# Block 0 of a linear-attention and SwiGLU kernel: k^T v in two parts, and the first weight piece moved behind k, v and q

## The chip, the cores and the metric

The kernel runs on one core of a Trainium2 chip. The metric is the device time of one execution in microseconds (us). The kernel before took 1027.06 us (median of three runs, 1026.48 to 1028.2).

A core has a matrix engine (PE, with its weight loads shown apart as PEld), a vector engine (DVE), a scalar engine (ACT), a pool engine (POOL), and a queue engine (SP) that in this kernel only issues transfers. Each engine works through its own list of instructions in order. Matrix results land in PSUM, which is taken in banks of 128 partitions by 512 float32.

## The reference

```
kv  = einsum('bhsd,bhse->bhde', k, v)          # 8 batches, 8 heads, 576 tokens, 64 wide
out = einsum('bhsd,bhde->bhse', q, kv)
rms = sqrt(mean(out*out, axis=-1) + 1e-06)
x   = (out / rms * g_norm)  -> transposed to (4608, 512)
y   = (silu(x @ w_gate) * (x @ w_val)) @ w_out # d_ff 1536
```

q, k, v and g_norm are float32. The three weights are float64 and are rounded to float32 on the chip.

## The kernel before

The 4608 tokens are handled in nine blocks of 512. For each block the attention part makes `x`, and the feed-forward part multiplies it with the weights. PE is busy nearly all the time, and what block n+1 needs of the attention part is done while block n is multiplied. Block 0 has nothing before it to hide behind, so its attention part lies open at the start of the kernel. The change is in that start, which `Att.first` (line 459) writes out in order.

**Loads.** `load_q(0)` (line 290) sends half of q of block 0. `load_first_kv` (line 221) then sends k and v in two halves `g` of four heads each: 512 KB of k and 512 KB of v per half on SP's queue (line 230), and two small pieces of 64 KB per half on ACT's queue (line 233). Line 234, inside that loop, asks for one weight piece, so the first piece of `w_gate` (512 KB, line 135) goes out between the first and the second half. Then `load_q(1)` sends the other half of q, and `load_weights(4)` three more pieces. Below, k1, v1 and k2, v2 are the two halves, and wg0, wv0, wg1, wv1, ... are the weight pieces in order: there are 24 of `w_gate` and `w_val`, then 12 of `w_out` (line 1036). Every transfer on these queues is given one of eight completion semaphores in turn and waits until the transfer that had that semaphore before it has landed.

**Room for loads.** The pool `ld` has four tiles. q takes two of them for a while, the weight pieces turn round in all four. A piece's tile is free for the next load once ACT (line 160) and DVE (line 152) have read it.

**Rounding a piece.** `begin` issues one ACT instruction (line 146) and three on DVE (lines 147, 152, 153); `finish` one on ACT (line 160) and one on DVE (line 162). `weights(n)` (line 1048) rounds pieces up to n. In block 0, wg0 is rounded by `weights(1)` right after q's first transposes, wv0 begins at line 468 and ends in `weights(2)`, and wg1 and wv1 come from `weights(3)` and `weights(4)` later.

**The attention part of block 0.** `turn_q(0)` transposes two tiles of q on PE. `first_kv` (line 239) computes k^T v for the four pairs of heads j into two banks of the pool `m` with 72 matmuls; each operand has 64 rows, and the two halves of the 128 tokens go to different banks, so the two banks must be added. ACT copies the first bank (line 253) and DVE adds the second (line 254). `product(0)` multiplies q with the sum (line 356), 32 matmuls; `turn_q(1)`, `product(1)`, the squares on ACT (line 367), their sums on DVE (line 368), the inverse root (`root`, small DVE instructions), the scaling (`scale`, line 113) and the transposes of x (`turn_x`, lines 403 and 404) follow. `warm` (line 484) keeps PE busy meanwhile. `plain_up` (line 1011) then multiplies x with the weights, first only for half of the tokens (`plain_up(0, (0,))`), and for one column tile f after another.

**Order.** The body of the kernel is recorded by a layer that orders the instructions of each engine by a planner's own estimates; `tc.issue_after(i)` keeps what is inside from being placed before instruction i. When a matmul reads a weight tile of which another part is rounded, the layer orders the two as if they overlapped: the matmuls with rows i = 1 to 3 of wg0 are made to wait for wg1 if wg1's rounding was recorded first.

**Towards block 1.** Once the weight piece number 30 has been sent, the loads of k, v and q of block 1 follow on SP's queue (line 265 and the 32 small transfers of line 283). q is transposed by DVE (line 330), and block 1's `product` waits for that.

Of the kernel before, what the change touches and what calls it, by code (L numbers as in the profile page):

```python
# [8 lines left out]
F32 = mybir.dt.float32  # L9
# [5 lines left out]
P = 128  # L15
# [3 lines left out]
def kernel(  # L19
# [41 lines left out]
    nc = tc.nc  # L61

    B, H, S, D = q.shape
# [7 lines left out]
    NS = DM // P  # L71
# [22 lines left out]
    a_psum = pool("a_psum", 1, space=PS)  # L94
    b_psum = pool("b_psum", 3, space=PS)
    c_psum = pool("c_psum", 2, space=PS)
    m_psum = pool("m_psum", 2, space=PS)
# [8 lines left out]
    kvs = [consts.tile([P, NS, D], F32, name=f"kv{i}") for i in range(3)]  # L106
# [4 lines left out]
    add = lambda e, o, a, b: e.tensor_tensor(out=o, in0=a, in1=b, op=OP.add)  # L111
# [62 lines left out]
    words = {}  # L174
# [18 lines left out]
    class Att:  # L193
# [27 lines left out]
        def load_first_kv(self):  # L221


            room = self.room.rearrange("p f (h x) -> p (f h) x", h=2)
            most = {"k": room[:, 0:H], "v": room[:, H : 2 * H]}
            last = {x: room[:, 2 * H + i].rearrange("p (h d) -> p h d", d=D) for i, x in enumerate("kv")}
            for g in range(2):
                heads, rows = slice(NS * g, NS * (g + 1)), slice(D * g, D * (g + 1))
                for x, src in (("k", k), ("v", v)):
                    nc.sync.dma_start(  # L230
                        out=most[x][:, heads], in_=src[0, heads, 0:BLK].rearrange("h (p t) d -> p h (t d)", t=T)
                    )
                    nc.scalar.dma_start(out=last[x][rows], in_=src[0, heads, BLK:S].rearrange("h p d -> p h d"))
                load_weights(1)
            self.k, self.v = (
                [most[x].rearrange("p h (t d) -> p h t d", t=T)[:, :, t] for t in range(T)] + [last[x]] for x in "kv"
            )

        def first_kv(self):

            banks = [m_psum.tile([P, NS, D], F32, name="m") for _ in range(2)]
            for j in range(NS):
                g = j // 2
                for c in range(T + 1):
                    for r in range(2) if c < T else (g,):
                        for u in range(2):
                            h = 2 * j + u
                            k, v = (t[c][r * D : (r + 1) * D, h if c < T else h % NS] for t in (self.k, self.v))
                            nc.tensor.matmul(
                                banks[r][u * D : (u + 1) * D, j], lhsT=k, rhs=v, start=(c == 0),  # L250
                                stop=(c == (T if r == g else T - 1)),
                            )
            nc.scalar.copy(out=kvs[0], in_=banks[0])
            add(nc.vector, kvs[0], banks[1], kvs[0])

        def load_kv(self, g):

# [84 lines left out]
        def product(self, i, pools=None):  # L342

            pools = pools or (m_psum, m_psum)
            self.ps[i] = [pool.tile([P, 2, NS, D], F32, name=pool.name[0]) for pool in pools]
            for t in range(2):  # L350
                for j in range(NS):
                    for b, _, p0, p1 in self.parts(2 * i + t):
                        for p in range(p0, p1, D):
                            for u in range(2):
                                rows = slice(u * D, (u + 1) * D)
                                self.multiplied = nc.tensor.matmul(  # L356
                                    self.ps[i][u][p : p + D, t, j, :],
                                    lhsT=self.qt[rows, 2 * i + t, j, p : p + D], rhs=kvs[b % 3][rows, j, :],
                                    start=True, stop=True,
                                )  # L360
            if self.z is None or 0 < self.n < TURNED:
                self.z = st_pool.tile([P, 2, 2, 2, NS], F32, name="z")
            if i == 0:
                self.sq = ring().rearrange("p f (t j d) -> p f t j d", t=2, j=NS)
            for u in range(2):
                sq = self.sq[:, 2 * i + u]
                self.squared = nc.scalar.activation(out=sq, in_=self.ps[i][u], func=ACT.Square)
                self.summed = nc.vector.tensor_reduce(out=self.z[:, i, u], in_=sq, axis=mybir.AxisListType.X, op=OP.add)
# [89 lines left out]

        def first(self):
            self.turn_q(0, (b_psum, c_psum))  # L460
            weights(1)
            self.first_kv()
            self.product(0)
            with tc.issue_after(self.multiplied.ins):
                self.turn_q(1, (b_psum, c_psum))

            with tc.issue_after(self.copied_q.ins), tc.issue_after(self.summed.ins):
                begun = words[pieces[1]].begin()
            with tc.issue_after(begun.ins):
                self.product(1, (b_psum, a_psum))  # L470
            self.warm()
            self.root(0, 2)
            self.scale(0)
            with tc.issue_after(self.squared.ins), tc.issue_after(self.scaled.ins):
                weights(2)
            self.turn_x(0)
            self.scale(1)
            return self.squared, self.scaled
# [561 lines left out]
    def load_weights(upto):  # L1040
        nonlocal loaded, sent
        while loaded < min(upto, len(pieces)):
            load_w(*pieces[loaded])
            loaded += 1
            if loaded == len(pieces) - NP:
                sent = words[pieces[loaded - 1]].sent

    def weights(upto):
        nonlocal rounded
        while rounded < min(upto, len(pieces)):  # L1050
            load_weights(rounded + 4 if blocks[0].q[2:] else 1)
            round_w(*pieces[rounded])
            rounded += 1

# [13 lines left out]
    for n in range(NB):  # L1068
        ffn = Ffn(n, blocks[n])
        nxt = blocks[n + 1] if n + 1 < NB else None  # L1070
        if n == 0:

            with tc.issue_after(squared.ins), tc.issue_after(scaled.ins):
                weights(3)
            ffn.plain_up(0, (0,))
            copied = blocks[0].copied
            blocks[0].turn_x(1)
            for f in range(NF):
                with tc.issue_after(blocks[0].copied.ins if f else copied.ins):
                    weights(2 * (f + 2))  # L1080
                ffn.plain_up(f) if f else ffn.plain_up(0, (1,))
            weights(len(pieces))
            pairs = wo.rearrange("p (j e) d -> p e j d", e=2)
            t2(pairs[:, 0, :, HD:DM], pairs[:, 1, :, HD:DM], pairs[:, 0, :, 0:HD])
            nxt.room = x_pool.tile([P, 3, 7, P], F32, name="xi").rearrange("p a b c -> p (a b c)")

            with tc.issue_after(sent.ins):
                for i in range(2):
                    nxt.load_kv(i)
                for i in range(2):  # L1090
                    nxt.load_q(i)
            ffn.plain_end()
            for g in range(2):
                nxt.kv(g)
        else:

            def third():
                nxt.kv(0)
                nxt.load_kv(1)

            def two_thirds():
                nxt.kv(1)
                if nxt.n == 2:
                    for i in range(2):
                        nxt.load_q(i)

            fill = {4: third, 8: two_thirds} if nxt else {}
            if n == DEEP:
                for a, at in enumerate((1, 2, 3, 5)):
                    fill[at] = lambda i=a // 2, j=a % 2: nxt.load_quarters(i, (j,))  # L1110
            ffn.up(fill)
        if nxt:
            nxt.turn()
        if 0 < n < NB - 2:
            blocks[n + 2].load_kv(0)
        if DEEP <= n < NB - 2:
            for i in range(2):
                blocks[n + 2].load_q(i)
        ffn.down(nxt)
        if n == 0:  # L1120
            blocks[2].load_kv(0)

            with tc.issue_after(nxt.halves[0].ins):
                for j in range(NP // 2):
                    t2(wv[j][:, 0:2], wv[j][:, 2:4], wg[j][:, 0:2])
            with tc.issue_after(ffn.down_.s4.ins):
                for j in range(NP // 2, NP):
                    t2(wv[j][:, 0:2], wv[j][:, 2:4], wg[j][:, 0:2])
# [31 lines left out]
```

## Time and profile before

| what | value |
|---|---|
| median of three runs | 1027.06 us |
| the profiled execution, its own time | 1028.2 us |
| its span, first to last instruction | 1026.4 us |
| PE busy | 1007.2 us (98%) |
| DVE busy | 702.3 us (68%) |
| ACT busy | 228.1 us (22%) |
| PE idle, 0 to 42 us, for k and v | 7.0 us in two waits |
| PE idle, 0 to 42 us, for q | 4.9 us in two waits |
| PE starts the 512-wide matmuls of block 0 | 41.33 us |
| mean granted PE clock | 1.00 |

The profile has several views. The chain of waits follows the work that ended last back to its start. The timeline lists instructions in order of time: start, length, engine, line, operation, output<-input, a count, and in brackets how long the engine had been idle and what ended that. Rows with "SPq" or "ACTq" are the issuing of transfers. A view by tile gives the shortest, median and longest duration of each kind of instruction in ns. PE waits of the start are the only long ones of the execution; after 42 us PE waits for other engines 2.1 us in all.

### The profile page before, as it was taken

Reading aid. Unit: us, or ns where it says so; the run is one execution under the profiler, and the core shown is the slowest. Engines: PE = TensorE matmul, PEld = TensorE weight load, DVE = VectorE, ACT = ScalarE, POOL = GpSimd, SP = SyncE. Lnnn points to the kernel's source line nnn. Section 1 sums busy time; section 2 is a strip of 40 time slices with the busy share of each in tenths; the row PEclk is TensorE's granted clock in tenths of the full one; section 3 lists DMA queues with packets and bytes.
Section 4 is the critical chain, followed back from the end, with each engine's and each line's share of the span. In section 5 each row is a group of like instructions: output and inputs, shape, how many; then the busy total and the mean of one; then the engine's idle time right before and its main releaser. Section 6 shows DMA issues by size and latency. Waiting matters only on the chain.

```text
span 1026.4 us, 21403 instructions
## 1 busy us (share of the span) xinstructions
PE 1007.2 (98%) x8522; PEld 897.9 (87%) x8522; DVE 702.3 (68%) x1168; ACT 228.1 (22%) x352; POOL 368.9 (36%) x280
## 2 busy tenths in 40 slices
PE   5999999999999999999999999999999999999998
PEld 4544688888999989998999899988999999989997
DVE  2998788998665855685657566664669466856661
ACT  2665211221112212221121121111112111211110
POOL 0000253445045512562156314730455036513670
PEclk9999999999999999999999999999999999999999
DMA  8589553567888466845686468737872766067601
GB/s 229 184 254 257 117 99 121 156 158 181 240 229 233 88 155 199 251 110 116 201 241 156 78 204 239 195 54 194 235 197 49 180 194 186 22 162 210 188 30 42
DMA packets 273844, 170.26 MB, mean 166 GB/s; under 512 B 150608, under 2 KB 241872, under 8 KB 273744
## 3 DMA queue, kind: packets, MB, share of 16 engines
q1 hardware_dynamic: 238800, 164.42, 59.1%
q10 hardware_dynamic: 34880, 4.46, 2.7%
q8 instruction: 68, 1.11, 0.5%
q14 instruction: 32, 0.26, 0.1%
q0 software_dynamic: 64, 0.00, 0.0%
HBM read 138.02 MB, written 22.41 MB: 156 GB/s over the span
## 4 chain that ended last, share of the span: by engine, by line
PE 89%; DVE 6%; DMA 3%; SPq 1%; issue 1%; ACT 0%; ACTq 0%; DVEq 0%
PE b L716 26%; PE b L553 19%; PE c L716 13%; PE c L553 10%; PE a L716 6%; PE a L553 5%; PE b L1020 4%; PE c L1020 4%; DMA h<-in_v_dram 1%; PE m L356 1%; PE m L315 1%; DVE r L112 1%; DVE r L111 1%; DVE xi L112 1%; SPq L283 1%
## 5 line engine op out<-in xcount | busy, mean ns | idle before, releaser
L111 POOL TENSOR_TENSOR r<-r 128x256 f32<-128x256 f32 (+1 forms) x105 | 110.7, 1061 | 301.1 <-DVE r L111 272.4
L111 DVE TENSOR_TENSOR r<-b,r 128x512 f32<-128x512 f32 (+1 forms) x273 | 161.9, 606 | 65.6 <-PE b L716 60.6
L112 POOL TENSOR_TENSOR t<-wo 128x512 f32<-128x512 f32 x81 | 114.5, 1437 | 217.0 <-DVE wo L111 108.6
L111 DVE TENSOR_TENSOR r<-c,r 128x512 f32<-128x512 f32 (+1 forms) x179 | 108.5, 617 | 88.2 <-PE c L716 54.5
L716 PE MATMUL b<-x,t 128*128 128x128 f32 x1092 | 151.3, 276 | 0.0
L111 DVE TENSOR_TENSOR r<-a,r 128x512 f32<-128x512 f32 (+1 forms) x99 | 62.5, 631 | 113.4 <-PE a L553 71.1
L716 PEld LDWEIGHTS b<-x,t 128*128 128x128 f32 x1092 | 136.5, 192 | 0.8 <-DVE r L111 0.2
L716 PE MATMUL c<-xi,t 128*128 128x128 f32 x840 | 112.4, 276 | 0.4 <-DVE xi L111 0.4
L113 POOL TENSOR_TENSOR h<-r 128x1024 f32<-128x1024 f32 (+1 forms) x40 | 82.3, 2072 | 77.0 <-DVE r L111 74.1
L716 PEld LDWEIGHTS c<-xi,t 128*128 128x128 f32 x840 | 102.9, 192 | 0.5 <-DVE xi L111 0.5
L553 PE MATMUL b<-wo,h 128*128 128x256 f32 x432 | 100.1, 383 | 0.1
L553 PE MATMUL b<-t,h 128*128 128x256 f32 x432 | 96.9, 381 | 0.0
L553 PEld LDWEIGHTS b<-t,h 128*128 128x128 f32 x432 | 81.6, 190 | 11.3 <-issue 0.2
L553 PEld LDWEIGHTS b<-wo,h 128*128 128x128 f32 x432 | 79.9, 190 | 13.1 <-DVE h L113 2.5
L730 ACT COPY r<-b 128x512 f32<-128x512 f32 x63 | 36.9, 585 | 211.6 <-PE b L716 206.5
L716 PE MATMUL b<-xi,t 128*128 128x128 f32 x588 | 79.8, 276 | 0.0
L716 PEld LDWEIGHTS b<-xi,t 128*128 128x128 f32 x588 | 72.4, 192 | 0.0
L716 PE MATMUL b<-x,wg 128*128 128x128 f32 x336 | 52.7, 279 | 0.2 <-DVE x L112 0.2
L716 PE MATMUL b<-x,wv 128*128 128x128 f32 x336 | 51.4, 276 | 0.0
L553 PE MATMUL a<-wo,h 128*128 128x256 f32 x216 | 48.3, 379 | 0.0
L553 PE MATMUL c<-wo,h 128*128 128x256 f32 x216 | 48.1, 379 | 0.0
L553 PE MATMUL c<-t,s 128*128 128x256 f32 x216 | 48.1, 379 | 0.0
(128 smaller groups left out, 1560.7 us busy)
## 6 DMA issues: line engine op xcount, KB each, us to landing
t<-w SPq DMA_DIRECT2D x336, 256.0 KB, 3.6
out_dram<-r SPq DMA_DIRECT2D x17, 512.0 KB, 3.1
ld<-in_k_dram SPq DMA_DIRECT2D x26, 288.0 KB, 4.9
ld<-in_v_dram SPq DMA_DIRECT2D x26, 288.0 KB, 6.1
ld<-in_moe_w_gate_dram SPq DMA_DIRECT2D x12, 512.0 KB, 4.6
ld<-in_moe_w_val_dram SPq DMA_DIRECT2D x12, 512.0 KB, 4.8
ld<-in_moe_w_out_dram SPq DMA_DIRECT2D x12, 512.0 KB, 5.6
w<-t SPq DMA_DIRECT2D x18, 256.0 KB, 3.0
```

Source lines behind the costliest of these rows:

```text
L111: add = lambda e, o, a, b: e.tensor_tensor(out=o, in0=a, in1=b, op=OP.add)
L112: sub = lambda e, o, a, b: e.tensor_tensor(out=o, in0=a, in1=b, op=OP.subtract)
L113: mul = lambda e, o, a, b: e.tensor_tensor(out=o, in0=a, in1=b, op=OP.mult)
L283: nc.sync.dma_start(out=to[32 * r : 32 * (r + 1), j, g0:g1], in_=q[b, 4 * i + 2 * j + h, s0 : s0 + 32 * (g1 - g0), 32 * d : 32 * (d + 1)]. ...
L315: nc.tensor.matmul(self.kv_ps[r][u * D : (u + 1) * D, g, :], lhsT=k[:, u, c, :], rhs=v[:, u, c, :], start=(c == 0), stop=(c == KT - 1),)
L356: self.multiplied = nc.tensor.matmul(self.ps[i][u][p : p + D, t, j, :], lhsT=self.qt[rows, 2 * i + t, j, p : p + D], rhs=kvs[b % 3][rows, ...
L553: nc.tensor.matmul(banks[e][:, e], lhsT=lhsT, rhs=rhs, start=first and i == 0 and (e == 0 or banks[0] is not banks[1]), stop=i == self.ste ...
L716: nc.tensor.matmul(ps[:, i, f], lhsT=self.weight(o, p, f), rhs=self.operand(o, p), start=first and (i, f) == (0, 0), stop=True, skip_group ...
L730: nc.scalar.copy(out=dst, in_=ps)
L1020: nc.tensor.matmul(t, lhsT=w[f // 2][:, i, P * (f % 2) : P * (f % 2 + 1)], rhs=x[:, i, of], start=(i == 0), stop=(i == NS - 1),)
```

## The change

Line 234 goes: no weight piece is sent between the halves of k and v, so the first four pieces all follow q. `weights(1)` goes from `first`, so the piece that is begun while block 0's second products are made is wg0, not wv0, and the rounding of each following piece moves one place later. k^T v is made in two calls, for pairs 0 and 1 and for pairs 2 and 3, each with two banks of its own (from pools `b` and `c`, then `b` and `a`), its own copy and its own addition of half the width. The products of q with pairs 0 and 1 are placed behind the last k^T v matmul, and those with pairs 2 and 3 behind these.

```diff
-                load_weights(1)
-        def first_kv(self):
-            banks = [m_psum.tile([P, NS, D], F32, name="m") for _ in range(2)]
-            for j in range(NS):
-                g = j // 2
+        def first_kv(self, g, pools):
+            banks = [pool.tile([P, 2, D], F32, name=pool.name[0]) for pool in pools]
+            for i in range(2):
+                j = 2 * g + i
 ...
-                            nc.tensor.matmul(
-                                banks[r][u * D : (u + 1) * D, j], lhsT=k, rhs=v, start=(c == 0),
+                            last = nc.tensor.matmul(
+                                banks[r][u * D : (u + 1) * D, i], lhsT=k, rhs=v, start=(c == 0),
                                 stop=(c == (T if r == g else T - 1)),
                             )
-            nc.scalar.copy(out=kvs[0], in_=banks[0])
-            add(nc.vector, kvs[0], banks[1], kvs[0])
+            dst = kvs[0][:, 2 * g : 2 * g + 2]
+            nc.scalar.copy(out=dst, in_=banks[0])
+            add(nc.vector, dst, banks[1], dst)
+            return last
 ...
         def product(self, i, pools=None):
-            pools = pools or (m_psum, m_psum)
-            self.ps[i] = [pool.tile([P, 2, NS, D], F32, name=pool.name[0]) for pool in pools]
+            self.heads(i, range(NS), pools or (m_psum, m_psum))
+            self.squares(i)
+        def heads(self, i, pairs, pools=None):
+            if pools:
+                self.ps[i] = [pool.tile([P, 2, NS, D], F32, name=pool.name[0]) for pool in pools]
             for t in range(2):
-                for j in range(NS):
+                for j in pairs:
 ...
         def first(self):
             self.turn_q(0, (b_psum, c_psum))
-            weights(1)
-            self.first_kv()
-            self.product(0)
+            self.first_kv(0, (b_psum, c_psum))
+            last = self.first_kv(1, (b_psum, a_psum))
+            with tc.issue_after(last.ins):
+                self.heads(0, (0, 1), (m_psum, m_psum))
+            with tc.issue_after(self.multiplied.ins):
+                self.heads(0, (2, 3))
+            self.squares(0)
 ...
-                begun = words[pieces[1]].begin()
+                begun = words[pieces[0]].begin()
 ...
-                weights(2)
+                weights(1)
 ...
     def weights(upto):
 ...
-            load_weights(rounded + 4 if blocks[0].q[2:] else 1)
+            load_weights(rounded + 4)
 ...
         if n == 0:
-                weights(3)
+                weights(2)
```

More of the change, by code (lines that the diff above doesn't have):

```diff
@@ L360, in product, with squares @@
                                 )
+        def squares(self, i):
             if self.z is None or 0 < self.n < TURNED:
```

## The prediction, made before the result was known

> **What bounds the kernel now.** I read the page first: PE is busy 98% of the span, so only work that stands between PE and its next matmul is worth anything, and after 42 us that is 2.1 us in all. So I turned to the chain of waits from 0 to 45 us. It runs through the second half of k and v, the k^T v matmuls, the addition of the two banks and the products:
>
> ```profile
> 6.31 10.00 DMA h<-in_v_dram
> 16.44 2.44 PE m L249 x72
> ...
> 18.98 0.43 DVE kv L111
> ...
> 19.45 1.98 PE m L356 x64
> 21.44 1.06 PE b L336 x4
> ```
>
> The last transfer of k and v takes 10 us, and PE idles 0.57 us between its last k^T v matmul (18.88) and the first product (19.45). The timeline of SP shows what is queued ahead of that transfer, and that of ACT when wg0 had landed:
>
> ```profile
> 2.88 0.51 SPq L230 DMA_DIRECT2D h<-in_v_dram  x1
> 4.79 0.37 SPq L135 DMA_DIRECT2D ld<-in_moe_w_gate_dram  x1
> 5.20 0.67 SPq L230 DMA_DIRECT2D h<-in_k_dram  x1
> 6.31 1.88 SPq L230 DMA_DIRECT2D h<-in_v_dram  x1
> 8.23 4.83 SPq L299 DMA_DIRECT2D ld<-in_q_dram  x2
> 13.11 2.97 SPq L135 DMA_DIRECT2D ld<-in_moe_w_val_dram  x1
> ```
> ```profile
> 13.29 0.69 ACT L146 ACTIVATE r<-ld 128x512 f32<-128x512 f32 x1 [8.37 <-DMA ld<-in_moe_w_gate_dram]
> ```
>
> The DMA engines are full meanwhile (by the windows, their busy share is 1.06 from 2 to 12 us and 1.08 from 12 to 16.4), so these transfers share one stream of bytes. The view by tile adds something that the page's clock row (1.00 throughout) does not show: PE's small matmuls of one shape get faster between 21 and 23 us.
>
> ```profile
> L356 PE MATMUL m<-kv,r x64: 310/311/365, 19.5 to 21.1; 64*64 64x64 f32 x64
> L356 PE MATMUL b<-kv,r x32: 217/218/268, 23.3 to 24.3; 64*64 64x64 f32 x32
> ```
>
> Last, the stage that follows. From 40 us DVE is as full as PE (20.00 of 20 us in the window 40 to 60), rounding weights; its idle spots before that, and the place where block 1 takes over, are in the timelines of DVE and SP:
>
> ```profile
> 37.76 0.42 DVE L113 TENSOR_TENSOR h<-h,c 128x256 f32<-128x256 f32 x1 [0.98 <-ACT h L1025]
> 38.89 0.43 DVE L147 TENSOR_SCALAR r<-r 128x512 f32<-128x512 f32 x1 [0.38 <-ACT r L146]
> 124.73 1.25 DVE L330 STREAM_TRANSPOSE r<-ld 128x1024 f32<-128x1024 f32 x1 [1.28 <-DMA ld<-in_q_dram]
> ```
> ```profile
> 103.00 20.03 SPq L283 DMA_DIRECT2D ld<-in_q_dram  x32
> ```
>
> The first of the 32 loads of q for block 1 waits for a tile that the rounding of `w_out` frees, not for PE; the last lands at 124.61, DVE transposes, and PE has waited 1.3 us (124.73 to 126.03) for its products. So whatever PE gains at the start counts only as far as DVE's rounding is early too.
>
> **The change, part by part.**
>
> *wg0 leaves the stream ahead of k2 and v2.* PE's first half of k^T v begins when v1 has landed, 11.90; wg0 is there at 13.29, so its 524 KB took 1.4 us. At the rate of the window 12 to 14 us (334 GB/s) they take 1.57. The lower bound is 0 (v2 lands when it does, whatever is ahead of it). The upper bound is 2.1: PE ends its first half at 14.30 (11.90 + 2.40) and the second began at 16.44. I take 1.5, by these two rows. SP's other steps move with it: k2 takes wg0's semaphore and can be issued at 4.79 instead of 5.20, v2 at 5.20 instead of 6.31, q at 6.31; with full queues that is worth nothing by itself. q's second half lands 1.5 earlier as well, and its transposes run later than that (21.37 before).
>
> *Two sums instead of one.* A copy of 128x256 (0.37) and an addition (0.42) become two copies and two additions of 128x128; ACT's two copies of that size at 119.32 take 0.43 together, DVE's additions of that size 0.29 each. The first pair, about 0.6 with its handoffs, lies under the second half's matmuls (2.4 us). The second pair has the products with pairs 0 and 1 as its cover: half of 1.98, that is 0.99 us, against 0.6. So the gap of 0.57 goes. Were the cover too short by the whole of it, the gap would stay; the row's other end is 0.57.
>
> *PE's faster rate comes earlier.* In this trace PE had run without a break from 19.45 when the change came (the transposes at 21.37 to 22.1 still take 421 ns, the last of the group at 22.9 takes 273), 3.3 us; its stretches of 2.4 us from 11.90 and 16.44 did not bring it. After the change the second half begins at about 14.9, the 0.57 gap is gone, and PE runs on: 3.3 us later is 18.2. The products then run from 17.3. Their 64 entries took 1.98 us at the slow rate and 1.27 (23.27 to 24.54) at the fast one; with 0.9 us at the slow rate, 0.4 is saved. The eight transposes of q took 1.81 (21.37 to 23.18) and take 1.06 at the fast rate (31.04 to 32.10). DVE's first copy waits for half of them and the rest of its chain for ACT, so I count 0.6 of the 0.75. Together 1.0. Bounds: 0 if the change of rate stays at 22.7, 2.1 if it comes at the start of the second half (0.85 of its 2.4, 0.7 and 0.6). The nearest row is the one unbroken stretch, so I take 1.0.
>
> The Trainium skill, "TensorE: Matmul & The Clock Gate", section "What's actually happening", says that the clock rises after one fully busy window of about 3.4 us and that this window is free-running. Where the trace has 3.3 us it agrees; its granted clock, 1.00 in every slice, does not show it. By that rule the rise could also fall up to one window later, at about 21.7, where it would bring next to nothing: the sum by it is anywhere between 1.6 and 2.6, not 2.6.
>
> *Up to the first x.* From `turn_q(1)` to the transposes of x (31.04) the lists are the same in kind and number; wg0 sits where wv0 sat: the same three DVE instructions ahead of the second sums, the same one between the scalings. So 31.04 becomes 31.04 - (1.5 + 0.57 + 1.0) = 28.0.
>
> *Column tile 0.* PE's order there becomes 8 transposes, 4 matmuls with wg0, 7 transposes, 4 with wv0, 1 transpose, then the other half. wv0 is now finished on DVE where wg1 was (34.55 + 0.69 = 35.24, less 3.1: 32.1); PE asks for it at 28.0 + 1.06 + 0.34 + 1.9 + 0.9 = 32.2. In return the matmuls with wg0 no longer wait for wg1 (they ran at 35.28 for that). Both of x's last copies on ACT stand behind the table load (1.28) and the small SiLU; that replaces the wait of 0.49 before 37.77. I count 0, with 0.5 either way.
>
> *DVE has a piece more to round.* wg0's four instructions lay in DVE's idle time from 13.29 to 16.0; now they are inside the busy stretch. By the spacing of such rows (0.34, 0.34, 0.60, 0.60) that is 1.88 us. DVE's two idle spots of 0.98 and 0.38 take up 1.36 of them: 0.52 is lost. Bounds: 0 and 1.88. wv1's load now has to wait until q's second tile is free (about 20.5 instead of 16.81); ACT wants it at about 31, and a piece takes 4.6 us to land by the page's row, so that is covered by 6 us.
>
> *Towards block 1.* PE enters the 512-wide matmuls 3.1 early and DVE's stream is 3.1 - 0.5 = 2.6 early, and with it the tiles that q's loads wait for. SP's 20 us of loads move as a whole. So block 1's products begin 2.6 early and PE's wait there grows from 1.3 to 1.8. Behind that the lists are unchanged, and PE's list is nearly without gaps.
>
> The sum is **2.6 us**: the profiled execution, 1028.2 (span 1026.4 and 1.8 around it), would take 1025.6. It lies 1.1 above the median of the runs, so I forecast 1027.06 - 2.6 = **1024.5 us**.
>
> **The rivals.**
> 1. *The rate does not rise earlier.* Then 1.0 goes: 1.5 + 0.57 - 0.52 = 1.55, 1025.5 us. For it: PE was busy in two stretches of 2.4 us without effect, and there is still a break of some 0.5 us at 14.4. Against it: 3.3 us unbroken was enough once.
> 2. *A wait takes the place of the one removed:* block 1's q does not come earlier, because DVE takes the whole 1.88 or the loads of k and v, during which the DMA engines are full (0.98 to 1.04 from 96 to 108 us), do not move. PE would wait at 124.7 for what it gained: 0 to 1.2 us of gain, about 1026.5. For it: the wait of 1.3 us is there already. Against it: the bytes are the same and begin earlier.
> 3. *Slower: wg0 comes late.* Its three DVE instructions stand ahead of the second sums, the root and the scaling, so DVE's whole chain waits for wg0. ACT wants it at 23.70 - 3.1 = 20.6. It is issued behind q, at about 11.6 to 14.6 (wv0's 13.11 to 16.08, less 1.5). The three pieces seen up to 30 us took 3.5 to 8.5 us to land, so between 15 and 23. Each us after 20.6 costs one; from 23.2 the gain is gone, from 25.3 the kernel is over 0.2% slower. A landing at 26 gives 1029.9. Against it: wv0, with 524 KB more ahead of it, was there at 23.70 with no wait of ACT.
>
> **How the numbers follow.** 0.2%, 2.05 us, is about what a measurement of this kernel can tell from no change. I give my forecast 0.68, the first rival 0.12, the second 0.08, the third 0.12. My forecast's own range is a gain of 1.6 to 4.2; some 0.04 of it lies under 2.05, while 0.02 of the first rival lies above. So faster 0.66, same 0.22, slower 0.12. The range reaches from a gain of 4.2 (2.1 instead of 1.0 for the rate, and 0.5 of DVE's loss not felt) to one of 0.5 in the second rival: 1022.8 to 1026.5.
>
> **What the profile would show.** PE's second k^T v half begins near 14.9 and the products follow without a gap; 218 ns products before 19 us; the transposes of x at 28.0; 512-wide matmuls from 38.2; the first q load of block 1 near 100.4 and its products at 123.4. A k^T v half that still begins after 16 refutes the first part, 311 ns in all first products the third, and an idle DVE before line 147 near 21 us speaks for the slow rival. A first q load that stays at 103 would make the sum wrong with all its early steps right.

## The result, and the profile after

| | median | runs | ratio to before, 95% interval |
|---|---|---|---|
| before | 1027.08 us | 1026.48 to 1028.2 | |
| changed, first measurement | 1023.24 us | 1023.18 to 1023.98 | 0.9963 [0.9946, 0.998] |
| changed, second measurement | 1024.35 us | 1022.57 to 1025.25 | 0.9975 [0.9965, 0.9985] |

The first measurement rests on four runs of each kernel. The second belongs to the experiment e5_after_again below and has eight runs beside 32 of before (median 1026.83). By ratio the change wins 3.8 us in the first and 2.6 us in the second. The forecast was a gain of 2.6, and 1024.5 us. In e1 below, one execution of eleven took 1156.07 us at a granted clock of 0.853, and e1's ratio is taken without it.

In the profiled execution of the changed kernel (1023.18 us, span 1021.4) the chain of waits at the start runs through the same stations as before. Columns are start, length, and what the chain went through:

```profile
4.92 8.82 DMA h<-in_v_dram
...
13.88 0.37 PE b L248 x2
...
15.85 0.12 PE a L248 x4
16.29 1.71 PE m L361 x57
17.99 0.73 PE b L337 x4
18.75 0.69 DVE r L341
```

The addition on DVE between k^T v and the products (line 111 in the chain of before) is gone from it: the products (line 361) follow the last k^T v matmul (line 248) directly. PE's waits from 0 to 42 us, with their sum, number and longest, say the same:

```profile
PE b L248 <- DMA h<-in_v_dram: 4.6, 2, 3.8
PE b L337 <- DMA ld<-in_q_dram: 4.3, 1, 4.3
PE b L1032 <- ACT x L411: 0.5, 2, 0.3
PE c L337 <- DMA ld<-in_q_dram: 0.4, 1, 0.4
PE b L361 <- DVE r L341: 0.4, 1, 0.4
```

Before, PE waited 7.0 us for k and v and 4.9 for q. Now it is 4.6 and 4.7. SP's timeline shows why. The loads of the second half follow those of the first, and the weight piece stands behind q:

```profile
2.85 0.51 SPq L230 DMA_DIRECT2D h<-in_v_dram  x1
4.51 0.37 SPq L230 DMA_DIRECT2D h<-in_k_dram  x1
4.92 0.74 SPq L230 DMA_DIRECT2D h<-in_v_dram  x1
6.36 4.33 SPq L300 DMA_DIRECT2D ld<-in_q_dram  x2
10.74 2.71 SPq L135 DMA_DIRECT2D ld<-in_moe_w_gate_dram  x1
```

By tile, with shortest, median and longest duration in ns, PE's rate in the products is still the slow one (311 ns, where 218 is the fast rate). It rises among the transposes of q behind them (421 ns is slow for these, 273 fast):

```profile
L361 PE MATMUL m<-kv,r x64: 310/311/366, 15.7 to 17.7; 64*64 64x64 f32 x64
L337 PE MATMUL b<-ident,ld x4: 273/284/454, 17.9 to 18.4; 128*128 128x128 f32 x4
```

At the passage to block 1, q's second half still makes DVE wait (0.70, where it was 1.28), but PE no longer waits for DVE:

```profile
119.20 1.25 DVE L331 STREAM_TRANSPOSE r<-ld 128x1024 f32<-128x1024 f32 x1 [0.70 <-DMA ld<-in_q_dram]
```
```profile
98.21 19.26 SPq L284 DMA_DIRECT2D ld<-in_q_dram  x32
```

Taken as a pair, the two first profiles differ by 5.0 us, more than either measurement. The profiled execution of before took 1028.2, 1.4 above the median of its later runs, and that of after was among the quick ones. So the path is better read from three profiles of each kernel.

### The profile page after: what moved, and what is told of

Its sections match the earlier page's. It is cut to its first block, busy times and chain, and to the rows that moved or that the text cites. A ratio compares the mean times of both kernels' runs of the same rounds, so it can differ in the third digit from the quotient of the medians.

```text
span 1021.4 us, 21409 instructions
## 1 busy us (share of the span) xinstructions
PE 1006.0 (98%) x8522; PEld 897.1 (88%) x8522; DVE 701.1 (69%) x1169; ACT 227.9 (22%) x353; POOL 369.0 (36%) x280
## 4 chain that ended last, share of the span: by engine, by line
PE 90%; DVE 6%; DMA 2%; issue 1%; ACT 1%; SPq 0%; DVEq 0%; ACTq 0%
PE b L728 26%; PE b L565 19%; PE c L728 13%; PE c L565 10%; PE a L728 6%; PE a L565 5%; PE b L1032 4%; PE c L1032 4%; PE m L316 2%; PE m L361 1%; DVE r L112 1%; DVE xi L112 1%; DVE r L111 1%; DMA h<-in_v_dram 1%; DVE t L112 1%
```

## Where the time went: one path in seven stretches

Every profile of this study can be laid out along the same marks on PE: the first matmul of the first and of the second half of k^T v, the first transpose of q's second half, the first transpose of x, the first 512-wide matmul, the first `b<-wo,h` matmul of block 0's down part, and the first such matmul behind block 1's products. The table has nine of the fourteen profiles; the other five come with their runs below. Distances in us between neighbouring marks:

| execution | first half begins | to second half | to q's transposes | to x's | to 512-wide | to down part | over block 1's products | span |
|---|---|---|---|---|---|---|---|---|
| before | 11.90 | 4.54 | 4.93 | 9.67 | 10.29 | 77.90 | 8.36 | 1026.4 |
| before (e9) | 10.94 | 4.63 | 4.92 | 9.71 | 10.29 | 77.90 | 8.31 | 1025.9 |
| before (e10) | 10.94 | 4.72 | 4.92 | 9.62 | 10.30 | 78.06 | 7.40 | 1024.8 |
| loads alone (e1) | 12.19 | 3.02 | 4.93 | 9.53 | 10.12 | 77.90 | 7.81 | 1024.7 |
| two parts alone (e2) | 10.62 | 4.74 | 4.05 | 9.57 | 10.30 | 78.05 | 7.40 | 1023.5 |
| changed | 10.69 | 3.19 | 4.05 | 9.23 | 10.11 | 77.90 | 7.41 | 1021.4 |
| changed (e5) | 10.91 | 3.32 | 4.05 | 9.86 | 10.09 | 77.91 | 7.40 | 1021.7 |
| changed (e11) | 11.17 | 3.07 | 4.06 | 9.65 | 10.11 | 77.90 | 8.81 | 1022.7 |
| two pieces between (e7) | 11.51 | 6.39 | 3.92 | 9.09 | 10.13 | 77.90 | 7.40 | 1024.8 |

Means of three, before against changed: second half 4.63 to 3.19 (1.44 won), q's transposes 4.92 to 4.05 (0.87), x's 9.67 to 9.58 (0.09), 512-wide 10.29 to 10.10 (0.19). These four make 2.59 us. The rest of the difference of the mean spans (1025.7 to 1021.9, 3.8) is 0.34 in the landing of the first half, 0.05 on the way to the down part, 0.15 in the wait of block 1 and 0.65 behind it. These vary within one kernel by as much or more: the landing by 1.0 in three profiles of before, the wait by 1.4 and the time behind it by 0.9 in three of after.

## The experiments

**Loads alone (e1_load_only).** The weight piece leaves the stream and its rounding moves one place, as in the change; k^T v stays in one part.

```diff
-                load_weights(1)
-            weights(1)
-                begun = words[pieces[1]].begin()
+                begun = words[pieces[0]].begin()
-                weights(2)
+                weights(1)
-            load_weights(rounded + 4 if blocks[0].q[2:] else 1)
+            load_weights(rounded + 4)
-                weights(3)
+                weights(2)
```

> Only the move of the loads and of the rounding; k^T v stays in one part with one sum, and all products wait for it. My theory (the stream of k and v is worth most): the second half of k^T v begins at 13.9 as in the changed kernel, 0.57 us of idle stands again ahead of the products, and the time is 0.6 us above the changed kernel's, about 1023.8. Rival (the split sums are what lets PE run on and reach its fast rate early, so they carry half): 1025 us or more, with the transposes of q at 421 ns again.

Measured: 0.9983 [0.9974, 0.9992], that is 1.7 us won of 1026.73. The timeline of PE, with idle time before a row and its releaser in brackets:

```profile
12.19 2.40 PE L248 MATMUL m<-h 64*64 64x64 f32 x72 [5.30 <-DMA h<-in_v_dram]
15.21 2.41 PE L248 MATMUL m<-h 64*64 64x64 f32 x72 [0.63 <-DMA h<-in_v_dram]
18.23 1.98 PE L359 MATMUL m<-kv,r 64*64 64x64 f32 x64 [0.60 <-DVE kv L111]
```

The second half begins 3.02 behind the first, and the gap of 0.60 ahead of the products stays. The theory had the second half at 13.9 and the time at 1023.8. The half came at 15.21, because the first one had landed late in this execution (12.19), and the median, 1025.13, is at the rival's bound; without the execution of 1156.07 it is 1024.9. Four of the eight transposes of q were still slow, as the rival said.

**Two parts alone (e2_split_only).** The new `first_kv(g, pools)` and `heads` as in the change, with the weight piece left between the halves.

```diff
-            self.first_kv()
-            self.product(0)
+            self.first_kv(0, (b_psum, c_psum))
+            last = self.first_kv(1, (b_psum, a_psum))
+            with tc.issue_after(last.ins):
+                self.heads(0, (0, 1), (m_psum, m_psum))
+            with tc.issue_after(self.multiplied.ins):
+                self.heads(0, (2, 3))
+            self.squares(0)
```

> Only the two parts of k^T v, with the first weight piece still sent between the halves and rounded early. My theory: the gap of 0.57 us goes and nothing else, about 1026.5. If the first weight piece is what delayed the FIRST half of k and v too (10.7 in the changed kernel, 11.9 before), the first half begins at 11.9 here; if that was chance between executions, it begins at 10.7 to 11. Rival (the split carries half of the gain): 1025 us.

Measured: 1025.45 us, 0.9990 [0.9981, 0.9999], 1.0 us won. That is nearer to the rival's 1025 than to the theory's 1026.5: more than the gap of 0.57 went. The first half began at 10.62, without any move of the loads. The distance between the halves is that of before (the row below begins 4.74 after the first half), and that from the second half to q's transposes that of after (4.05). The products are all slow:

```profile
15.36 0.37 PE L249 MATMUL b<-h 64*64 64x64 f32 x2 [2.34 <-DMA h<-in_v_dram]
```
```profile
L362 PE MATMUL m<-kv,r x64: 311/311/365, 17.1 to 19.2; 64*64 64x64 f32 x64
```

So the two halves of the change act on different stretches of the path, and in each run the other's stretch stayed as it was before (4.93 and 4.74). The load's move shortens "to second half" and, by 0.18, "to 512-wide"; the two parts shorten "to q's transposes". The two gains in time, 1.7 + 1.0, make 2.7, beside 2.6 in the second measurement; as each is known only to about 0.9 either way, it is the stretches that show it.

**The changed kernel again (e5_after_again).** No edit.

> The changed kernel once more, timed beside the same runs of the kernel before as the three that follow. If the two halves of the change add up, its gain is the sum of what each half alone gave beside 1026.73 us: 1.60 (loads alone, 1025.13) + 1.28 (two parts alone, 1025.45) = 2.88, that is 1023.85. If each half also frees something that the other alone cannot use, the first measurement stands: 1023.24, a gain of 3.5 or more. Rows: whatever the first half's landing is in this execution, the second half of k^T v 3.0 to 3.2 us after it, the products at once behind it, no idle PE ahead of block 1's second products.

Measured: 1024.35 us, 0.9975 [0.9965, 0.9985]. The sum of the halves in that text, 1023.85, is taken with e1's slowest execution in its median; by the ratios it is a gain of 2.7. That lies nearer to the 2.6 measured than a gain of 3.5 does, but the interval (1.5 to 3.6 us) just holds 3.5 too, so an interplay of the halves in the time is not excluded.

**Two pieces between the halves (e7_after_two_pieces).** The changed kernel, with the cause put back twice.

```diff
                     nc.scalar.dma_start(out=last[x][rows], ...)
+                load_weights(2)
```

> The changed kernel with the first two weight pieces (512 KB) loaded between the k, v of the two halves, where the kernel before has one (256 KB); the rounding stays as changed. Theory (the loads up to the second half share one stream, and 256 KB of it cost 1.5 us): the second half comes 3.1 + 3.0 = 6.1 us after the first, transposes of x 3.0 later than in the changed kernel, PE's idle stretch ahead of the second half grows to 3.8 and takes the fast rate of the transposes of q with it (0.75), and the time is 1023.2 + 3.0 to 3.75, 1026.2 to 1027. Rival (what was gained was the landing of that execution, not the 256 KB): less than 4.6 between the halves and a time under 1024.7.

(The sizes in that text are half of the true ones. The profile's issue rows give 512 KB for one piece, so 1 MB for the two.) Measured: 1026.65 us, 1.0001 [0.9992, 1.001], and on PE:

```profile
11.51 0.37 PE L249 MATMUL b<-h 64*64 64x64 f32 x2 [4.80 <-DMA h<-in_v_dram]
17.90 0.37 PE L249 MATMUL b<-h 64*64 64x64 f32 x2 [3.99 <-DMA h<-in_v_dram]
```

6.39 between the halves, against 3.19 without a piece: 1.6 us for each. The whole time rises by 2.3 over the second measurement of the changed kernel. Of the 3.2 us, 0.6 comes back in the two stretches behind (3.92 and 9.09, against 4.05 and 9.58), so nearly all of the other 2.6 comes through to the end. One row was not as expected: the transposes of q did not lose the fast rate. It came 3.7 us after 17.90, within the last products.

**PE kept busy ahead of k^T v, in both kernels (e3_after_fill, e12_after_fill_again, e4_before_fill).** 16 (changed) or 20 (before) matmuls whose result nobody reads fill the time in which PE waits for the first half.

```diff
+            ps = a_psum.tile([P, NS, P], F32, name="a")
+            for _ in range(16):
+                nc.tensor.matmul(ps[:, 0], lhsT=ident, rhs=ident, start=True, stop=True)
```

> The changed kernel with 16 idle-time matmuls of 128x128 added between q's first transposes and k^T v, where PE waits for k and v; their result is not used. Theory (PE's rate rises after some 3.3 to 4 us without a break): k^T v's second half and the first products run at 218 ns instead of 311, 0.8 + 0.7 us earlier, and x is ready 1.5 us earlier; if the weight stream follows, about 1021.8. Rival (block 1's q sets the pace from here on, since its last transposes end only 0.2 us before PE wants them): x comes 1.5 earlier, the end does not, 1023 us. If the rate does not change the small matmuls, 1023.2 with all at 311 ns.

> The kernel before with 20 such matmuls in the same place, and nothing else changed. Theory: fast rate from k^T v on, 0.85 + 0.7 + 0.6 = 2.1 us earlier at the transposes of x, unless the idle time of 2.1 us between the halves takes the rate back; about 1025.0 if block 1's q follows. Rival (block 1's q is tied to the weight stream, not to x): x earlier, but PE's wait for block 1's q grows by as much, 1027 us.

> The changed kernel with the 16 filling matmuls ahead of k^T v once more. In its first profile the stretch from the second half's begin to the transposes of q took 3.00 us (4.05 in three profiles of the changed kernel) and that from there to the transposes of x 9.10 (9.23, 9.86, 9.65): 1.5 less by PE's rate alone. If PE's start sets the end, 1.0 to 1.5 under the changed kernel's second measurement (1024.35): 1022.9 to 1023.4, and the first measurement, 1023.51, is repeated or bettered. If what PE wins at the start is taken back in the wait for block 1's q, the transposes of x come 1 us or more earlier, there is an idle stretch of PE of as much ahead of block 1's second products, and the time is 1024.0 to 1024.6.

Measured: e3 1023.51 us, 0.9969 [0.9958, 0.998]; e12 1023.64, 0.997 [0.996, 0.998]; e4 1027.79, 1.0008 [0.9999, 1.0017]. The rate does follow the filling. By tile, the products of e3:

```profile
L361 PE MATMUL m<-kv,r x64: 218/218/267, 15.6 to 17.4; 64*64 64x64 f32 x64
```

No time came near the theories' 1021.8 (e3) and 1025.0 (e4); both lie nearer to the rivals' 1023 and 1027. From the second half to q's transposes e3 and e12 take 3.00 and 2.95 (4.05 without filling), and from there to x's 9.10 and 9.09 (9.58 in the mean). The down part begins at 114.71 and 114.61, 1.1 earlier than in the mean of the changed kernel's three profiles. Of that, a part is given back where block 1's products end: both have an idle spot there that the profile puts down to no other engine or transfer of data ("issue"), and the filled version of before has a longer one. PE's timeline of e3, e12 and e4:

```profile
122.11 0.70 PE L568 MATMUL b<-wo,h 128*128 128x256 f32 x2
123.06 1.13 PE L568 MATMUL b<-wo,h 128*128 128x256 f32 x4 [0.25 <-issue]
```
```profile
122.53 0.70 PE L568 MATMUL b<-wo,h 128*128 128x256 f32 x2
123.62 0.70 PE L568 MATMUL b<-wo,h 128*128 128x256 f32 x2 [0.39 <-issue]
```
```profile
125.45 0.27 PE L356 MATMUL b<-kv,r 64*64 64x64 f32 x1 [1.37 <-issue]
```

In e12 the wait for block 1's q takes 0.5 more (7.92 over block 1's products instead of 7.40). Behind the last mark, the stop included, e3 and e12 take 899.2 and 899.3, and the changed kernel took 897.9 to 898.8. So neither case expected for e12 came whole: the first ended at 1023.4 and the second began at 1024.0. The medians are 1023.5 and 1023.6 with filling, 1023.2 and 1024.4 without; the intervals overlap, and no version of this study is shown to beat the changed kernel. In e4, x comes at 28.43 (30.20 to 31.04 without filling), and the rival's row, a longer wait for block 1's q, is not there; in its place stands the stop of 1.37. That execution (1026.24) is one of the quickest of its eleven, whose median is 1027.79, so what the others lose is in no profile and stays open.

The trace's list of transfers says more of these stops than the views do. In all fourteen profiles there are six of over 0.1 us: the three above, 0.17 us in e3 and 0.12 in e12 at 16.9 us, and 1.31 in e8 below. Each ends 1.30 to 1.50 us after a transfer of kind "instruction" (queue q8, 16 KB) has ended, and q8 has only 68 of these in a whole execution. The likely reading is that PE had run out of instructions and waited for the next ones; no run tests it.

**DVE later by eight instructions (e8_after_dve_delay).** The changed kernel; the added clamps change no value.

```diff
                 ffn.plain_up(f) if f else ffn.plain_up(0, (1,))
+                if 2 < f < 11:
+                    nc.vector.tensor_scalar(
+                        out=ffn.h[:, f - 1], in0=ffn.h[:, f - 1], scalar1=-1e30, scalar2=1e30, op0=OP.max, op1=OP.min
+                    )
```

> The changed kernel with 8 more DVE instructions (128x512 in place on finished parts of h, a clamp that changes nothing) among block 0's up products: 8 times 0.34 to 0.42 us, 2.7 to 3.4 us of DVE in the stretch where it is busy all the time, five times what the prediction said of one more piece in it (0.52). Theory of the prediction (DVE's rounding sets when block 1's q is loaded, and q sets PE's second products): the first load of q 2.7 to 3.4 later than 98.2, the second transposes at 122, PE's products idle 2.1 to 2.8 ahead of the second half (0.6 of slack in the changed kernel: transposes end at 120.45, PE comes to them at 121.07), and the time 1025.3 to 1026. Rival (DVE has slack there, as the changed kernel's rows, in which the piece more cost nothing, suggest): the load of q less than 1 us later and the time 1023.2 to 1023.5.

Measured: 1026.8 us, 1.0009 [0.9997, 1.0021]. SP's first load of block 1's q, DVE's second transposes and PE's second products:

```profile
102.75 18.93 SPq L284 DMA_DIRECT2D ld<-in_q_dram  x32
```
```profile
123.41 1.25 DVE L331 STREAM_TRANSPOSE r<-ld 128x1024 f32<-128x1024 f32 x1 [2.19 <-DMA ld<-in_q_dram]
```
```profile
124.71 0.27 PE L361 MATMUL m<-kv,r 64*64 64x64 f32 x1 [2.29 <-DVE r L331]
```

The load begins 3.5 later than the mean of the changed kernel's three profiles (99.24), PE waits 2.29, and the stretch over block 1's products is 9.92 instead of 7.40. The theory's rows came as written. The time came 0.8 above its range; this profile also has a stop of 1.31 at 18.5 us, once more one of the kind "issue", which DVE's added work, far behind it, did not cause:

```profile
19.84 0.55 PE L337 MATMUL c<-ident,ld 128*128 128x128 f32 x3 [1.31 <-issue]
```

**Block 1's q on two queues (e6_before_q_two_queues).** The kernel before.

```diff
+                            by_act = self.n == 1 and i == 1 and r % 2
-                            nc.sync.dma_start(
+                            with tc.issue_after(self.lit.ins) if by_act else ExitStack():
+                                (nc.scalar if by_act else nc.sync).dma_start(
 ...
-            nc.scalar.activation(out=h, in_=ps[0], func=ACT.Silu)
+            self.lit = nc.scalar.activation(out=h, in_=ps[0], func=ACT.Silu)
```

> The kernel before with 8 of the 32 loads of block 1's q issued on ACT's queue behind its last silu of block 0, the other 24 on SP as ever; everything else as before. In the profile of before the 32 take SP 20.03 us (0.63 each), the second part of q comes 1.28 us after DVE is ready for it, and PE's products wait 0.72 and start 0.94 later than they could. Theory (this wait was on the path before the change and is a part of what the change won): 24 loads take 15.0, q is there some 3 us sooner, the wait is gone, the distance from the first b<-wo,h row to the second of block 0's down falls from 8.36 to 7.4, and the time by 0.95, to 1025.8. Rival (the wait costs nothing, its time is lost again behind it): the distance falls but the time stays at 1026.7. Second rival: the loads on ACT hold up its copies of block 1's k^T v, and the time rises.

Measured: 1027.63 us, 1.0005 [0.9996, 1.0013]. The issue rows of SP and ACT:

```profile
100.38 21.40 SPq L285 DMA_DIRECT2D ld<-in_q_dram  x24
```
```profile
114.05 3.87 ACTq L285 DMA_DIRECT2D ld<-in_q_dram  x8
```

The 24 loads left on SP took 21.40, not 15.0: 0.89 each. So SP's time is not a price per instruction; the loads wait for tiles and landings, as the waits of SP's queue in the first profile of before also have it. On ACT eight took 0.48 each. PE's wait was gone as expected (7.41 over block 1's products). The time did not fall with it. That is the first rival's reading, but the profile shows no later place where the 0.95 is lost; the start of that execution was late (first half at 11.77, x at 31.39), in part because PE's rate rose only at 25.1 us, 2.2 to 3.1 later than in the three profiles of before. It stays open.

**Second and third profiles (e9_before_look, e10_before_look2, e11_after_look).** No edit.

> The kernel before once more, for a second profile: the profile shown of it took 1028.2, and the 32 timed runs beside the last four kernels have a median of 1026.83, so that execution was 1.4 late. If the landing of the first half's k, v is what differs from execution to execution (10.5 to 12.2 in ten profiles), this one shows the first half nearer to 11.0, the second 4.5 behind it, and the end that much earlier. If the landing goes with the one-part form of k^T v (11.77 to 12.19 in four profiles with it, 10.53 to 11.51 in six without), it is at 11.8 or later again, and what differs is the wait for block 1's q: under 0.9 of idle PE, where the first profile had 0.94.

> The kernel before a third time, as the run ahead of it; two more landings tell better than one whether 11.8 to 12.2 belongs to the one-part form or to chance.

> The changed kernel a third time. Landing by form: 10.5 to 11.0 again; landing by chance: anywhere from 10.5 to 12.2. Second half 3.0 to 3.4 behind the first in either case. The rise of PE's rate: 4.1 to 5.1 after the second half's begin if it comes at a step that runs on its own, always at one distance if it counts busy time.

Measured, one execution each: 1027.66, 1026.53 and 1024.43 us. PE's two halves in e9, e10 and e11:

```profile
10.94 2.40 PE L249 MATMUL m<-h 64*64 64x64 f32 x72 [4.12 <-DMA h<-in_v_dram]
15.57 1.72 PE L249 MATMUL m<-h 64*64 64x64 f32 x53 [2.23 <-DMA h<-in_v_dram]
```
```profile
10.94 2.40 PE L249 MATMUL m<-h 64*64 64x64 f32 x72 [4.02 <-DMA h<-in_v_dram]
15.66 1.65 PE L249 MATMUL m<-h 64*64 64x64 f32 x50 [2.32 <-DMA h<-in_v_dram]
```
```profile
11.17 0.37 PE L248 MATMUL b<-h 64*64 64x64 f32 x2 [4.42 <-DMA h<-in_v_dram]
14.24 0.37 PE L248 MATMUL b<-h 64*64 64x64 f32 x2 [0.68 <-DMA h<-in_v_dram]
```

The landing of the first half does not go with the form of k^T v: in one part it was 11.77 to 12.19 in the executions up to e8, and is 10.94 twice here. These three ran on another chip than e1 to e8, so whether it differs by execution or by chip is not separated. In e9 it came 0.96 earlier than in the first profile, and the span is only 0.5 shorter. The wait for block 1's q differs within one kernel on one chip: e9 has it (8.31), e10 not (7.40), and e11, the changed kernel, has it again:

```profile
123.21 0.27 PE L361 MATMUL m<-kv,r 64*64 64x64 f32 x1 [1.17 <-DVE r L331]
```

## Why the prediction was right, and which steps were not

The forecast of 1024.5 us is 1.3 above the first measurement and 0.15 above the second, and its gain of 2.6 equals the second's. The four stretches that the change moves in every profile also make 2.6. But the terms of the sum did not all come as written.

- *wg0 leaves the stream, 1.5:* 1.44 in the means of three, 1.52 with this half alone against before's first profile, and 1.6 for each of two pieces put back. The row used (524 KB in 1.4 us behind the first half) was the right one.
- *Two sums instead of one, 0.57:* the gap is gone in every profile with two parts and stays, 0.60, with the loads alone. The stretch won 0.87, not 0.57. Before, the second half's 2.41 and the products' 1.92 (to the next transposes) make 4.33 without the gap; in the changed kernel both together take 4.05. The prediction had treated the products as following k^T v, but they start ahead of its last matmuls. In the trace of before the last four groups of k^T v (18.22 to 18.55) have two matmuls each, 0.107 us apart, where the earlier ones have four: the second half's extra pieces all go to one bank. In the changed kernel the first products start in that time:

```profile
15.66 0.37 PE L361 MATMUL m<-kv,r 64*64 64x64 f32 x1
15.76 0.32 PE L248 MATMUL a<-h 64*64 64x64 f32 x2
15.82 0.31 PE L361 MATMUL m<-kv,r 64*64 64x64 f32 x1
15.86 0.31 PE L248 MATMUL a<-h 64*64 64x64 f32 x1
```

- *PE's faster rate comes earlier, 1.0:* this is the step that failed. The products stayed at 311 ns in all three profiles of the changed kernel, so the 0.4 counted there never came. The stretch to x's transposes gave 0.44 in the first profile and nothing in the other two: 0.09 in the mean of three, against 0.6. The prediction took "3.3 us after an unbroken start" from one row of one execution, as if it were a fixed time.

  The traces hold a record of the granted clock that settles this. It begins only when the rate rises; the views show 1.00 for the time before, in which there is no record. It begins at 22.88, 22.11 and 22.02 us in the three profiles of before and at 18.22, 19.90 and 19.07 in those of the changed kernel: 4.3, 5.7 and 4.8 us after the second half's begin, from which on PE runs with hardly a break (0.03 us at most). Behind the break of 0.6 ahead of the products it is 2.9 us in e1, 3.4 to 3.5 in the three profiles of before and 5.5 in e6. In all fourteen profiles the record lasts, up to the fall to 0.50 at the end, a whole number (293 to 298) of steps of 3.413 us. PE stands still for at most 0.55 us in the step that ends with the rise (e1), and for 0.60 us or more in the step before it (e6 has 0.60). As far as these profiles go, the rise waits for the end of a step in which PE is busy all but some 0.55 us, and the steps run on whether PE works or not. How long that takes then depends on where in a step PE starts, and this differs between executions of one program.

  That the fast rate is worth what was said is shown by e3 and e12, whose record begins at 8.87 and 11.53, ahead of the products: 1.1 us less from the second half to q's transposes and 0.5 less from there to x's. The Trainium skill, "TensorE: Matmul & The Clock Gate", section "What's actually happening", has the window in which activity is watched run freely; the steps of 3.413 us agree with it. The prediction gave "between 1.6 and 2.6" for the sum by that rule, because the rise could come up to one window of about 3.4 us later. The measured 4.3 to 5.7 lies within one to two such windows, so the rule's spread should have gone into the sum, not beside it. So the first rival named what happened, in the mean; its time, 1025.5, was too high because other terms came out better.
- *Column tile 0, 0 ± 0.5:* 0.19 won, and e1 and e2 put it to the move of the weight piece (10.12 against 10.30).
- *DVE has a piece more to round, -0.52, and PE's wait for block 1's q grows from 1.3 to 1.8:* the down part begins 2.97 earlier in the mean of three profiles, the first load of q 2.47 earlier (101.71 to 99.24). That is a loss of 0.5 on DVE's side, but the loads of one kernel lie 2.0 to 2.3 apart, so the agreement shows little. The 1.3 was a misreading to begin with: it runs from the begin of DVE's transposes (124.73), while PE itself stood still for only 0.72 of it. And the wait did not grow: 0.96, 0.91 and 0 before, 0, 0 and 1.41 after (what the stretch over block 1's products has above 7.40). The step that failed is taking one execution's wait as a fixed one. The mechanism behind it is right, as e8 showed: a DVE that is 3.5 later makes PE wait and the end late. Over the profiles with all 32 loads on SP's queue and no stop of the other kind there, PE does not wait when the first load comes 16.9 or more ahead of the down part, with e9 (16.99, wait 0.91) as the exception; its loads took longest, 22.3 us from the first issue to the last landing, and 20.5 to 21.9 in the others.
- *Rival 2, q takes the place of the gain:* excluded by the measurements as a rule; e11 is an execution in which it took 1.4 of it.
- *Rival 3, wg0 late:* ACT begins it at 19.70, ahead of the 20.6 at which it was wanted, and the row has no wait:

```profile
19.70 0.69 ACT L146 ACTIVATE r<-ld 128x512 f32<-128x512 f32 x1
```

In sum: 1.44 for 1.5, 0.87 for 0.57, 0.09 for 1.0, 0.19 for 0, and in the mean no cost from DVE for -0.52. The total was right because an expected gain that did not come (0.9) was offset by a cost that did not come either (0.5) and by two small gains (0.3 + 0.2). That these errors cancelled is luck; the loads' term was right in mechanism and size, that of the two sums in mechanism.

## What to carry to other kernels

Where the start of a kernel waits for a full stream of loads, ask what stands in front of the awaited one: here 512 KB cost 1.4 to 1.6 us, with one piece or with two. A sum of two banks can be hidden by making it in two parts and giving PE the work that needs only the first; what it wins is read from the distance between two marks on PE, not from the idle row alone. One profile of each kernel is not enough for terms of half a microsecond: the landing of a first load and a wait 100 us later moved by 1.0 to 1.4 us between executions of one program, so a stretch that is the same in three profiles is evidence, and one that differs is not. A gain that hangs on when PE's rate rises is a draw, and belongs into a forecast as a spread.

## What was not expected of the hardware

- 64x64 matmuls took 311 ns at the slow rate and 218 at the fast one, 128x128 transposes 421 and 273. From start to start the difference is larger: transposes follow each other in 0.213 us (before) and 0.109 (e3), groups of four 64x64 matmuls in 0.107 and 0.059. The views show a granted clock of 1.00 in both, because the trace's record of it begins with the rise.
- PE stood still for 0.25 to 1.37 us in e3, e4, e8 and e12 with no releaser in the profile, in e3 and e12 at the same instruction. In e4 the DMA engines were full around the stop (their packets took 104% of the 16 engines' time from 123.5 to 126 us), in e8 the stop lasted on while they emptied (56% from 18.5 to 19.84). What all of them share is a 16 KB instruction transfer that had ended 1.30 to 1.50 us before PE went on.
- Taking 8 of 32 small loads off SP's queue did not shorten SP's part (20.03 us for 32, 21.40 for 24, one execution each).
